# Channel MLP in a fused FAVOR / gated-MLP / mixer kernel: the c additions ahead in VectorE's order, weight sums and last differences on VectorE, the second group's cw loads in pieces, u of the first chunk asked for earlier

## The chip, the cores and the metric

The kernel runs on one core of a Trainium2 chip. The metric is the time of one execution in device microseconds (us). The timed runs of the kernel before gave 1591.82, 1593.74 and 1594.99 us, with the median at 1593.74 us; these come from executions without a profile. One further execution was profiled, and everything said of engines below is from that one.

## The reference

Three stages follow each other, all in float32, over a batch of 8 with 576 tokens and 512 features. The first is a linear attention with exponential features, the second a gated MLP whose gate mixes the tokens, the third a mixer, of which the last part is the channel MLP that this change is about.

```python
def _moe2_ref(x, U, V, w_ch1, w_ch2):
    xt = x.transpose(0, 2, 1)
    h = xt @ U @ V
    u = x + h.transpose(0, 2, 1)
    ch = np.maximum(u @ w_ch1, 0.0) @ w_ch2
    return (u + ch).astype(np.float32)

def reference(**kwargs):
    attn_out = _attn_ref(**attn_kwargs)                # 8 x 8 heads x 576 x 64
    x = np.ascontiguousarray(attn_out.transpose(0, 2, 1, 3)).reshape(B, S, H * D)
    x = _moe_ref(x=x, **moe_kwargs)                    # gated MLP, 512 -> 1024 -> 512
    return _moe2_ref(x=x, **moe2_kwargs)               # low rank token mix, then 512 -> 2048 -> 512
```

## The kernel before

TensorE (PE) works in single-pass float32 (fp32r). Each fp32 operand is split into a rounded part and a rest, and a product of two operands is three matmuls (method `products`, L873). The split (method `split`, L184 to L187) is a cast on ScalarE (ACT) for the rounded part, and a subtraction on VectorE (DVE) for the rest, called the low part below.

**The channel MLP** works through 16 chunks n. A chunk is one batch (576 tokens) with one half of the 2048 hidden features: chunks 0 to 7 take the first group of four weight blocks m (128 x 2 columns each), chunks 8 to 15 the second group. Both matrix products of a chunk are done by a Strassen-like scheme with 7 instead of 8 block products (tables `PRODUCTS` and `OUTER`), so operands need sums and differences of their blocks first. In detail:

- **The right parts** of the first product (method `right_parts`, tiles `t`, `us`): differences of the blocks of the mixer's output u, on GpSimd (POOL, method `less`, L1245), split into `us0` to `us6`. For chunk 0, `first_chunk` (L1241) loads u from the scratch tensor `ud`, and the generator `first_parts` hands out the parts step by step.
- **The first product** (generator `hidden`, tiles `ph_x`, `ph_y`, `ph_z`): 7 products for each weight block, with weights `cw` that `load_left` (L1182) brings in, one load of 1792 KB for each block. DVE adds what PE left in PSUM to copies that ACT made (`c`, L1317). The addition that matters here is the one in `plus(Y, u3, True)`: product 5 of the same block writes into the same bank `ph_z`, so PE must wait until this addition has read it. It is not emitted where it arises, but handed to `inner` as a function (`after`), which `inner` calls one slot later, behind what that slot's caller put on DVE.
- **The second product** (method `channel`, tiles `pc`): operands `hc` (split from the hidden values `h` or their differences `t2`, made by `sums` through `less` on POOL), weights `w` loaded from `w2d` (`outer_weights`, L1449). Its results are added to `r` on DVE (`more`, L1481), stored to `pd` between the groups, and to `outT` at the end.
- **The second group's weights** are prepared while chunks 0 to 6 run (generator `second_group`): 8 blocks, for each four raw 128x256 pieces (tile `ca`), four sums and differences on POOL (`left_sums`, L548, tile `cs`), then splits (tile `cd`, ACT cast and DVE low part) and stores to `w1x` or `w2d` (L1228).

PE runs the two products interleaved, slot by slot: six matmuls of a `ph`, then six of a `pc`, and so on; a chunk has 28 slots of each. Two slots of the table `order` in `inner` are done early: chunk 0's first blocks run in between the last batch's gated output, its low-rank step (`pr`, operands `xh` and `xl`, L1060 and L1062) and its mixing step. The gated MLP and this transition are inside a manual schedule, and the order of instructions on each engine is the order in which the code emits them. DMAs are issued by SyncE (SP) alone, which works in order: a load that waits holds what stands behind it.

`inner` decides by two tables, `begin` (for chunk 1) and `spread` (for the others), at which slots the right parts of the next chunk are made; in the chunk that ends the first group, it calls `load_left` for the four blocks of the second, at slot 6 of each block.

## Time and profile before

| | us |
|---|---|
| timed runs, median (range) | 1593.74 (1591.82 to 1594.99) |
| the profiled execution, own time | 1598.42 |
| the profiled execution, span of the trace | 1596.6 |
| attention (start to about 375) | 375 |
| gated MLP, 8 batches (375 to about 835) | 460 |
| transition and channel MLP (835 to the end) | 762 |

| engine | busy us | share of the span |
|---|---|---|
| PE | 1556.6 | 97% |
| PE weight loads | 1467.3 | 92% |
| DVE | 1133.2 | 71% |
| ACT | 875.8 | 55% |
| POOL | 812.0 | 51% |

PE is the engine that is nearly always busy. In a trace like this, the time that a change can give back is the time that PE does not work or works at the lower of its clock levels, and both are read from PE's rows: each row has its start, its length and in brackets the idle time ahead of it and the instruction that ended it. The granted clock stands in a column of its own in the table of stretches, 1.00 being full speed (2.4 GHz) and 0.5 the lower level (1.2 GHz); a value between says that the stretch had both.

### The profile page before, as it was taken

The page shows a single profiled execution, that of the slowest core. Times are in us where ns is not written, and L with a number is a line of the kernel's source. Part 1 is how long each engine was busy: PE and PEld are TensorE (multiplying, and loading weights), DVE is VectorE, ACT ScalarE, POOL GpSimd, SP SyncE. Part 2 cuts the span into 40 slices and gives each one's busy share as a digit, 9 for nine tenths or more (in the row PEclk, how much of TensorE's full clock was granted, in tenths as well). Part 3 has the DMA queues.
Part 4 walks back from the last instruction along what each step waited for, and adds up shares of the span by engine and source line. Part 5 has one row for each costly group of instructions (what it writes and reads, how often), then busy time and mean ns, then how long its engine had stood idle before and what let it go on. Part 6 is the DMA issues. An engine that isn't in the chain of part 4 may idle for free.

```text
span 1596.6 us, 30554 instructions
## 1 busy us (share of the span) xinstructions
PE 1556.6 (97%) x11592; PEld 1467.3 (92%) x11592; DVE 1133.2 (71%) x1628; ACT 875.8 (55%) x1656; POOL 812.0 (51%) x610
## 2 busy tenths in 40 slices
PE   7999999999999999999999999999999999999998
PEld 7998889988898898898898999999999999999998
DVE  5888767884686787787676767777766666666656
ACT  4878777784444454454445555555544555555542
POOL 2677776766344454453332645455644543434433
PEclk9999999999999999999999999999999999999999
DMA  4677676763243454452328888988989877777786
GB/s 130 172 212 205 195 199 174 205 173 110 83 159 109 129 178 145 139 181 94 110 88 318 258 290 281 317 289 293 311 311 389 259 248 235 237 242 245 248 250 230
DMA packets 172278, 336.87 MB, mean 211 GB/s; under 512 B 25826, under 2 KB 96610, under 8 KB 169060
## 3 DMA queue, kind: packets, MB, share of 16 engines
q1 hardware_dynamic: 171988, 334.86, 65.5%
q8 instruction: 91, 1.49, 0.4%
q14 instruction: 55, 0.45, 0.1%
q10 hardware_dynamic: 144, 0.07, 0.0%
HBM read 251.73 MB, written 73.55 MB: 204 GB/s over the span
## 4 chain that ended last, share of the span: by engine, by line
PE 80%; DMA 8%; DVE 5%; ACT 3%; issue 2%; SPq 1%; POOL 0%; DVEq 0%; ACTq 0%; POOLq 0%
PE pc L873 18%; PE ph_x L873 11%; PE pu L873 6%; PE pz L873 6%; PE pv L873 6%; PE ph_z L873 6%; PE px L873 5%; PE pn L706 4%; PE pkv L678 4%; PE ph_y L873 3%; DMA w<-w2d 2%; PE pk L605 2%; PE pt L637 1%; PE pt L1082 1%; PE pz L1008 1%
## 5 line engine op out<-in xcount | busy, mean ns | idle before, releaser
L873 PE MATMUL pc<-hc,w 128*128 128x288 f32 x2688 | 424.0, 295 | 4.8 <-DMA w<-w2d 2.0
L873 PEld LDWEIGHTS pc<-hc,w 128*128 128x128 f32 x2688 | 379.7, 188 | 6.2 <-ACT us L184 2.0
L659 POOL TENSOR_TENSOR qp<-e,qp 128x576 fp32r<-128x576 f32 x128 | 183.6, 1456 | 119.5 <-ACT e L656 87.3
L873 PE MATMUL ph_x<-us,cw 128*128 128x288 f32 x1536 | 243.0, 296 | 1.1 <-ACT u L1312 0.6
L873 PEld LDWEIGHTS ph_x<-us,cw 128*128 128x128 f32 x1536 | 217.0, 188 | 2.3 <-ACT u L1312 1.4
L706 PE MATMUL pn<-qp,kv 128*65 128x288 f32 x768 | 208.3, 332 | 8.0 <-DVE nd L715 4.4
L187 DVE TENSOR_TENSOR hc<-h,hc 128x576 fp32r<-128x576 f32 x192 | 189.0, 987 | 35.4 <-ACT hc L184 35.3
L1245 POOL TENSOR_TENSOR h<-h,h 128x576 f32<-128x576 f32 x64 | 109.2, 1708 | 132.4 <-DVE r L1481 126.2
L1245 POOL TENSOR_TENSOR t<-u,t 128x576 f32<-128x576 f32 x32 | 56.4, 1762 | 194.9 <-DVE c L1317 179.7
L678 PE MATMUL pkv<-v,kp 128*128 128x65 f32 x1024 | 154.2, 254 | 0.0
L678 PEld LDWEIGHTS pkv<-v,kp 128*128 128x128 f32 x1024 | 152.9, 193 | 0.0
L1312 ACT COPY u<-ph_x 128x288 f32<-128x288 f32 x128 | 51.1, 399 | 184.6 <-PE ph_x L873 184.6
L873 PE MATMUL ph_z<-us,cw 128*128 128x288 f32 x768 | 123.3, 296 | 10.1 <-DVE c L1317 10.1
L184 ACT CAST hc<-h 128x576 fp32r<-128x576 f32 x192 | 128.5, 672 | 6.5 <-PE pc L873 3.6
L1327 ACT ACTIVATE h<-c 128x288 f32<-128x288 f32 x192 | 85.2, 444 | 85.1 <-DVE c L1317 85.0
L873 PEld LDWEIGHTS ph_z<-us,cw 128*128 128x128 f32 x768 | 108.4, 188 | 12.3 <-DVE c L1317 12.2
L706 PEld LDWEIGHTS pn<-qp,kv 128*65 128x65 f32 x768 | 100.1, 141 | 14.1 <-DVE nd L715 6.0
L873 PE MATMUL pz<-wt,vn 128*128 128x288 f32 x768 | 112.0, 295 | 0.0
L873 PEld LDWEIGHTS pz<-wt,vn 128*128 128x128 f32 x768 | 105.3, 188 | 0.0
L1481 DVE TENSOR_TENSOR r<-pc,r 128x576 f32<-128x576 f32 x111 | 83.7, 754 | 30.2 <-PE pc L873 29.6
L873 PEld LDWEIGHTS pu<-xs,wi 128*128 128x128 f32 x768 | 102.7, 188 | 0.7
L873 PE MATMUL pu<-xs,wi 128*128 128x288 f32 x768 | 103.2, 295 | 0.0
(162 smaller groups left out, 3076.2 us busy)
## 6 DMA issues: line engine op xcount, KB each, us to landing
w<-w2d SPq DMA_DIRECT2D x224, 512.0 KB, 4.7
u<-ud SPq DMA_DIRECT2D x16, 1152.0 KB, 8.3
raw_c<-in_w_ch SPq DMA_DIRECT2D x32, 512.0 KB, 3.8
cw<-w1x SPq DMA_DIRECT2D x8, 1792.0 KB, 14.5
v<-in_v SPq DMA_DIRECT2D x32, 325.0 KB, 4.2
k<-in_kT SPq DMA_DIRECT2D x32, 320.0 KB, 3.6
q<-in_qT SPq DMA_DIRECT2D x32, 320.0 KB, 3.9
x<-nd SPq DMA_DIRECT2D x64, 144.0 KB, 3.3
```

Source lines behind the costliest of these rows:

```text
L184: self.put(nc.scalar.copy(hi, src))
L187: return self.put((nc.gpsimd if elo == "pool" else nc.vector).tensor_tensor(out=lo, in0=src, in1=hi, op=ALU.subtract))
L605: self.pin(nc.tensor.matmul(pa[:, j * NF + t, :], x[d, t * P : (t + 1) * P], ws[d, :], start=True, stop=True,))
L637: self.pin(nc.tensor.transpose(pt[:, at, :], s[:, u, :], self.ident))
L659: self.pin(nc.gpsimd.tensor_tensor(out=lo[:, c], in0=e[:, c], in1=hi[:, c], op=ALU.subtract))
L678: self.pin(nc.tensor.matmul(pkv[:, i, j, :], kp[:, j * NF + t, :], vb[:, u * D1 : (u + 1) * D1], start=False, stop=(j == 1 and t == NF - 1),))
L706: self.pin(nc.tensor.matmul(pn, kv[k][:, i, g // 2, :], qp[q][:, i, g * HS : (g + 1) * HS], start=(m == 0), stop=(m == len(terms) - 1),))
L873: self.put(self.nc.tensor.matmul(out, x, y, start=(start and i == 0), stop=(stop and i == len(terms) - 1), skip_group_check=chained,))
L1245: x = self.put(self.nc.gpsimd.tensor_tensor(out=out, in0=p, in1=q, op=ALU.subtract))
L1312: self.put(nc.scalar.copy(out, src))
L1327: self.put(nc.scalar.activation(self.h[n, t // 2, x][:, t % 2], src, AF.Relu))
L1481: self.read = self.put(nc.vector.tensor_tensor(out=r, in0=pc, in1=r, op=ALU.add)).ins
```

## The change

- `first_chunk` is called in the last batch's `gate`, behind the batch's last `pu` products, when its home (tile `xs`) is free; before, it was called when the gate was done.
- `first_parts` hands out the first chunk's right parts in another order and more in each step, so that `us0`, `us4`, `us1` and `us2` stand ahead of the `xh` and `xl` of the low-rank step.
- The addition of `ph_z` and `u3` is marked urgent: `inner` holds it in `self.urgent`, and `hurry` emits it at the head of the next slot or of the next `pc` product, ahead of the `hc` parts, rather than behind them.
- The four sums of each of the 8 blocks are made on DVE instead of POOL. The raw pieces and the sums share one tile `c32`, the splits one tile `cd`, both in the pool `cst`.
- The second group's `cw` come in four pieces for each block (two of 512 KB, two of 384 KB), one asked for at every second slot. Block 4 gets a home of its own, in `c32` and `cd`; block 5 takes the home of block 0, and so on.
- In the last chunk the differences of the hidden values are made on DVE instead of POOL, and the bank pair of the last chunk's first `pc` product is two banks of the tag "a", each added by an instruction of its own.
- The table `begin` makes chunk 1's right parts some slots earlier.

```diff
         )):
-            self.put(self.nc.gpsimd.tensor_tensor(out=z[:, x], in0=p, in1=q, op=op))
+            self.put((engine or self.nc.gpsimd).tensor_tensor(out=z[:, x], in0=p, in1=q, op=op))
...
         loads = [load(kk) for kk in range(2)]
+        if b + 1 == self.B:
+            self.u0 = self.first_chunk()
         gs = self.gs if b == 0 else self.gated(b)
...
                 self.alloc_channel(ctx)
-                u = self.first_chunk()
                 for m in range(GROUP):
                     self.load_left(m)
-                right_parts = self.first_parts(u)
+                right_parts = self.first_parts(self.u0)
                 inner = self.inner()
...
             begun = [self.gated_open(b, t) for t in range(3)]
-            parts(3)
+            parts(4)
             self.work(b, "x")
...
                 ts.append(self.gated_out(b, t, begun[t] if t < 3 else None))
-                parts(1)
+                if t >= 2:
+                    parts(1)
                 if t == 1:
...
-    def load_left(self, m):
+    def load_left(self, m, whole=True):
         g, t = divmod(m, GROUP)
-        w = self.cw.tile([P, 2, 7, 2, P], F32R, tag=f"w{t}", name=f"cw{m}", bufs=1)
-        self.nc.sync.dma_start(
-            w.bitcast(F32).rearrange("p i x k c -> p i x (k c)"), self.w1x[g][:, t]
-        )
-        self.w1[m] = w
+        dma = self.nc.sync.dma_start
+        if whole:
+            w = self.cw.tile([P, 2, 7, 2, P], F32R, tag=f"w{t}", name=f"cw{m}", bufs=1)
+            dma(w.bitcast(F32).rearrange("p i x k c -> p i x (k c)"), self.w1x[g][:, t])
+            self.w1[m] = [w[:, i] for i in range(2)]
+            return
+        if t == 0:
+            self.w1[m] = [
+                self.cst.tile([P, 16 * P], F32R, tag=tag, name=f"cw{m}_{tag}", bufs=1)[:, : 14 * P]
+                .rearrange("p (x k c) -> p x k c", x=7, k=2) for tag in ("c32", "cd")
+            ]
+        else:
+            w = self.cw.tile([P, 2, 7, 2, P], F32R, tag=f"w{t - 1}", name=f"cw{m}", bufs=1)
+            self.w1[m] = [w[:, i] for i in range(2)]
+        def load(i, x):
+            dma(
+                self.w1[m][i].bitcast(F32)[:, x].rearrange("p x k c -> p x (k c)"),
+                self.w1x[g][:, t][:, i, x],
+            )
+        self.pieces += [
+            lambda i=i, x=x: load(i, x) for x in (slice(0, 4), slice(4, 7)) for i in range(2)
+        ]
...
     def fetch_raw(self, kind, m):
-        a = self.cst.tile([P, 4, 2 * P], F32, tag="c32a", name=f"ca{kind}_{m}", bufs=1)
+        a = self.c32[:, 0].rearrange("p (x c) -> p x c", x=4)
         return self.raw_blocks(a, kind, m)
-    def sums_of(self, a, name):
-        z = self.cst.tile([P, 4, 2 * P], F32, tag="c32s", name=f"cs{name}", bufs=1)
-        self.left_sums([a[:, x] for x in range(4)], z)
+    def sums_of(self, a):
+        z = self.c32[:, 1].rearrange("p (x c) -> p x c", x=4)
+        self.left_sums([a[:, x] for x in range(4)], z, self.nc.vector)
         return z
...
         blocks = [(kind, m) for kind in (1, 2) for m in range(GROUP, self.NM)]
+        self.c32 = self.cst.tile([P, 2, 8 * P], F32, tag="c32", name="c32", bufs=1)
+        self.cd, made = self.cst.tile([P, 2, 8 * P], F32R, tag="cd", name="cd", bufs=1), 0
         raw = self.fetch_raw(*blocks[0])
...
             t, a = m - GROUP, raw
-            z = self.sums_of(a, f"{kind}_{m}")
+            z = self.sums_of(a)
             yield
             for x, k, src in ((0, 2, a[:, :2]), (2, 1, a[:, 2:3]), (3, 2, z[:, :2]), (5, 2, z[:, 2:])):
-                d = self.w2p.tile([P, 2, 2, 2 * P], F32R, tag="cd", name=f"cd{kind}_{m}_{x}", bufs=2)
+                d = self.cd[:, made % 2].rearrange("p (i k c) -> p i k c", i=2, k=2)
+                made += 1
                 self.split(d[:, 0, :k], d[:, 1, :k], src, elo="dve")
...
-    def less(self, out, p, q, after=None):
-        x = self.put(self.nc.gpsimd.tensor_tensor(out=out, in0=p, in1=q, op=ALU.subtract))
+    def less(self, out, p, q, after=None, engine=None):
+        engine = engine or self.nc.gpsimd
+        x = self.put(engine.tensor_tensor(out=out, in0=p, in1=q, op=ALU.subtract))
         if after is not None:
...
         parts = self.right_parts(0, u)
-        for names in (("t1", "t2"), (0,), (4,), (2,), ("t3",), (1,), ("t6",), (3,), (6,), (5,)):
+        for names in (("t1", "t2", 0), ("t3", 4), (1,), ("t6", 2), (3,), (6,), (5,)):
             for x in names:
...
         c22 = []
-        yield lambda: c22.append(plus(Y, u3, True))
+        def add():
+            c22.append(plus(Y, u3, True))
+        add.urgent = True
+        yield add
         product(X, 6, False, True)
...
         begin = {
-            (1, 4): ("t1", "t2"), (2, 2): ("t3",), (2, 3): (0,), (2, 6): (4,), (3, 2): (1, "t6"),
-            (3, 3): (2,), (3, 4): (3,), (4, 0): (6,), (3, 6): (5,),
+            (1, 4): ("t1", "t2"), (2, 0): ("t3",), (2, 1): (0,), (2, 2): (4,), (2, 3): (1, "t6"),
+            (2, 4): (2,), (2, 5): (3,), (2, 6): (6,), (3, 6): (5,),
         }
...
                 late = None
+            self.hurry()
             after = next(pairs[k])
...
             late = after
+            if getattr(after, "urgent", False):
+                self.urgent, late = after, None
             if (t, i) == (1, 0) and n + 1 < groups * B:
...
                 right.pop(x)()
-            if i == 6 and (n + 1) % B == 0 and g + 1 < groups:
-                self.load_left((g + 1) * GROUP + t)
+            if (n + 1) % B == 0 and g + 1 < groups and (i == 6 and t < GROUP - 1 or (t, i) == (0, 0)):
+                self.load_left((g + 1) * GROUP + (t + 1 if i else 0), False)
+            if self.pieces and i % 2 == 0:
+                self.pieces.pop(0)()
             yield
+        self.hurry()
         if late:
             late()
+    def hurry(self):
+        f, self.urgent = self.urgent, None
+        if f:
+            f()
...
         b11, b12, b21, b22 = (self.h[n, q, i] for i in range(4))
+        last = n + 1 == self.NM // GROUP * self.B
+        engine = self.nc.vector if last else None
         if x == 1:
-            self.less(b11, b12, b11, after)
+            self.less(b11, b12, b11, None if last else after, engine)
         elif x == 2:
             self.t2[n, q] = self.hc.tile([P, 2, self.HS], F32, tag="t2", name=f"t2{n}_{q}", bufs=2)
-            self.less(self.t2[n, q], b22, b11)
+            self.less(self.t2[n, q], b22, b11, engine=engine)
         elif x == 3:
-            self.less(b12, b22, b12)
+            self.less(b12, b22, b12, engine=engine)
         else:
-            self.less(b21, b21, self.t2[n, q])
+            self.less(b21, b21, self.t2[n, q], engine=engine)
...
             r = rs[n, i, j]
+            if isinstance(pc, list):
+                for f in range(2):
+                    self.put(nc.vector.tensor_tensor(out=r[:, f], in0=pc[f], in1=r[:, f], op=ALU.add))
+                return
             self.read = self.put(nc.vector.tensor_tensor(out=r, in0=pc, in1=r, op=ALU.add)).ins
...
                 if x in (0, 4, 2):
-                    pc = banks(f"pc{n}_{x}", "x" if x == 0 else "y")
+                    if x == 0 and n + 1 == total:
+                        pc = [self.psum(f"pc{n}_{x}_{f}")[:, :HS] for f in range(2)]
+                    else:
+                        pc = banks(f"pc{n}_{x}", "x" if x == 0 else "y")
                     if x == 0:
...
                             r = rs[n, 1, 0][:, f]
-                            self.put(nc.vector.tensor_tensor(out=r, in0=X[:, f], in1=r, op=ALU.add))
+                            self.put(nc.vector.tensor_tensor(out=r, in0=X[f], in1=r, op=ALU.add))
                             store(n, 1, 0, (f,))
...
                 for t in range(GROUP):
+                    self.hurry()
                     if t % 2 == 0:
...
                         self.products(
-                            pc[:, f],
+                            pc[f] if isinstance(pc, list) else pc[:, f],
                             [([w[:, t % 2, i, f * P : (f + 1) * P] for i in range(2)],
```

On DVE, at the start of the channel MLP, the order before was this (`us` are right parts, `xh` and `xl` the operands of the low-rank step):

```order
L187 TENSOR_TENSOR us0_0_9742<-u32_0_9698,us0_0_9742 128x576
L187 TENSOR_TENSOR us4_0_9745<-u32_0_9698,us4_0_9745 128x576
L186 CAST xh7_0_9749<-x_7_0_9748 128x512
L187 TENSOR_TENSOR xl7_0_9750<-x_7_0_9748,xh7_0_9749 128x512
L187 TENSOR_TENSOR us2_0_9757<-t1_0_9738,us2_0_9757 128x576
L186 CAST xh7_1_9761<-x_7_1_9760 128x512
L187 TENSOR_TENSOR xl7_1_9762<-x_7_1_9760,xh7_1_9761 128x512
L186 CAST xh7_2_9771<-x_7_2_9770 128x512
L187 TENSOR_TENSOR xl7_2_9772<-x_7_2_9770,xh7_2_9771 128x512
L187 TENSOR_TENSOR us1_0_9779<-t2_0_9740,us1_0_9779 128x576
L186 CAST xh7_3_9783<-x_7_3_9782 128x512
L187 TENSOR_TENSOR xl7_3_9794<-x_7_3_9782,xh7_3_9783 128x512
```

The order after the change:

```order
L187 TENSOR_TENSOR us0_0_9742<-u32_0_9512,us0_0_9742 128x576
L187 TENSOR_TENSOR us4_0_9746<-u32_0_9512,us4_0_9746 128x576
L187 TENSOR_TENSOR us1_0_9749<-t2_0_9740,us1_0_9749 128x576
L187 TENSOR_TENSOR us2_0_9753<-t1_0_9738,us2_0_9753 128x576
L186 CAST xh7_0_9757<-x_7_0_9756 128x512
L187 TENSOR_TENSOR xl7_0_9758<-x_7_0_9756,xh7_0_9757 128x512
L186 CAST xh7_1_9766<-x_7_1_9765 128x512
L187 TENSOR_TENSOR xl7_1_9767<-x_7_1_9765,xh7_1_9766 128x512
L186 CAST xh7_2_9775<-x_7_2_9774 128x512
L187 TENSOR_TENSOR xl7_2_9776<-x_7_2_9774,xh7_2_9775 128x512
L187 TENSOR_TENSOR us3_0_9783<-u32_0_9512,us3_0_9783 128x576
L186 CAST xh7_3_9787<-x_7_3_9786 128x512
```

The right parts `us1` and `us2` moved ahead of all `xh` and `xl`, and `us3` from behind them to ahead of the last two.

On DVE, in chunk 1 (products `pc1` beside `ph2`), around the addition of block 1, which is the row `c2_1` with `u32_1`, before:

```order
L187 TENSOR_TENSOR hc1_1_0_10970<-t21_0_10888,hc1_1_0_10970 128x576
L187 TENSOR_TENSOR cd1_5_0_11002<-ca1_5_10427,cd1_5_0_11002 128x512
L187 TENSOR_TENSOR cd1_5_2_11007<-ca1_5_10427,cd1_5_2_11007 128x256
L187 TENSOR_TENSOR hc1_1_1_11017<-t21_1_10967,hc1_1_1_11017 128x576
L1317 TENSOR_TENSOR c2_1_11037<-ph2_1_z_10981,u32_1_11000 128x288
```

After the change:

```order
L187 TENSOR_TENSOR hc1_1_0_10964<-t21_0_10882,hc1_1_0_10964 128x576
L187 TENSOR_TENSOR cd_10254<-c32_10253,cd_10254 128x512
L187 TENSOR_TENSOR cd_10254<-c32_10253,cd_10254 128x256
L1341 TENSOR_TENSOR c2_1_11008<-ph2_1_z_10975,u32_1_10994 128x288
L187 TENSOR_TENSOR hc1_1_1_11010<-t21_1_10961,hc1_1_1_11010 128x576
```

The addition moved from behind `hc1_1_1` to ahead of it; the two `cd` rows still stand ahead.

On DVE, in chunk 0 (products `pc0` beside `ph1`), around the addition of block 3, `c1_3` with `u31_3`, before:

```order
L1317 TENSOR_TENSOR c1_3_10659<-ph1_3_y_10652,s11_3_10604 128x288
L187 TENSOR_TENSOR us1_2_10680<-t2_2_10543,us1_2_10680 128x576
L187 TENSOR_TENSOR hc0_5_1_10689<-h3_0_2_10182,hc0_5_1_10689 128x576
L187 TENSOR_TENSOR us2_2_10707<-t1_2_10531,us2_2_10707 128x576
L1481 TENSOR_TENSOR r0_11_10328<-pc0_0_10262,r0_11_10328 128x576
L187 TENSOR_TENSOR us3_2_10726<-u32_2_10341,us3_2_10726 128x576
L187 TENSOR_TENSOR hc0_6_0_10729<-h2_0_0_9910,hc0_6_0_10729 128x576
L1317 TENSOR_TENSOR c1_3_10749<-ph1_3_z_10700,u31_3_10724 128x288
```

After the change:

```order
L1341 TENSOR_TENSOR c1_3_10654<-ph1_3_y_10647,s11_3_10602 128x288
L187 TENSOR_TENSOR us1_2_10675<-t2_2_10540,us1_2_10675 128x576
L548 TENSOR_TENSOR c32_10253<-c32_10253 128x256 x4
L187 TENSOR_TENSOR hc0_5_1_10683<-h3_0_2_10188,hc0_5_1_10683 128x576
L187 TENSOR_TENSOR us2_2_10701<-t1_2_10528,us2_2_10701 128x576
L1527 TENSOR_TENSOR r0_11_10331<-pc0_0_10263,r0_11_10331 128x576
L187 TENSOR_TENSOR us3_2_10720<-u32_2_10342,us3_2_10720 128x576
L1341 TENSOR_TENSOR c1_3_10723<-ph1_3_z_10694,u31_3_10718 128x288
L187 TENSOR_TENSOR hc0_6_0_10725<-h2_0_0_9910,hc0_6_0_10725 128x576
```

Four sums (`c32<-c32`, one row, x4) came in ahead of the addition, and `hc0_6_0` went behind it. Chunk 5 has its second block of sums at the same place.

On SP, in chunk 6's second product, around the last store of a split (`w2d1<-cd`), before:

```order
L1449 DMA w2_6_3_1_14037<-w2d0_87 128x1024
L1449 DMA w2_6_5_0_14079<-w2d0_87 128x1024
L1228 DMA w2d1_88<-cd2_7_5_14112 128x2x256 x2
L1449 DMA w2_6_5_1_14120<-w2d0_87 128x1024
L1182 DMA cw6_14156<-w1x1_90 128x3584
L1449 DMA w2_6_6_0_14161<-w2d0_87 128x1024
L1449 DMA w2_6_6_1_14204<-w2d0_87 128x1024
L1494 DMA pd6_84<-r6_11_13893 128x2x288
L1449 DMA w2_7_0_0_14244<-w2d0_87 128x1024
```

After the change:

```order
L1199 DMA cw6_13977<-w1x1_90 128x1024
L1491 DMA w2_6_5_0_14044<-w2d0_87 128x1024
L1199 DMA cw6_13977<-w1x1_90 128x768 x2
L1251 DMA w2d1_88<-cd_10254 128x2x256 x2
L1491 DMA w2_6_5_1_14086<-w2d0_87 128x1024
L1199 DMA cw7_14122<-w1x1_90 128x1024
L1199 DMA cw4_cd_13645<-w1x1_90 128x1024
L1199 DMA cw4_cd_13645<-w1x1_90 128x768
L1491 DMA w2_6_6_0_14127<-w2d0_87 128x1024
L1199 DMA cw7_14122<-w1x1_90 128x1024
L1491 DMA w2_6_6_1_14171<-w2d0_87 128x1024
```

Of block 4, the half that lies in `cd` is asked for right behind the last store out of `cd`; the pieces of blocks 6 and 7 stand between the `w2` loads one at a time.

## Rows read from the trace of the kernel before

**Rows 1.** Waits of PE from 835 us on: us in total, times, longest.

```profile
PE ph_z L873 <- DVE c L1317: 10.1, 9, 2.6
PE pc L873 <- DMA w<-w2d: 2.0, 2, 1.8
PE pc L873 <- DVE r L1481: 1.3, 2, 0.9
```

**Rows 2.** Stretches: span, busy us of PE, PEld, DVE, ACT, POOL, clock, DMA.

```profile
851.00:855.50 4.50, 4.32 (x20) 3.92 (x20) 4.26 (x7) 1.55 (x3) 1.54 (x1) 0.62 0.99 421
884.00:888.50 4.50, 4.50 (x25) 4.50 (x24) 3.34 (x6) 3.35 (x8) 0.13 (x1) 0.63 0.66 215
1164.00:1259.00 95.00, 90.63 (x680) 89.77 (x679) 61.84 (x85) 47.23 (x102) 40.01 (x24) 1.00 0.92 330
1259.00:1526.00 267.00, 267.00 (x2021) 267.00 (x2020) 169.13 (x241) 137.31 (x294) 119.48 (x72) 1.00 0.79 246
```

**Rows 3.** Timeline, transition: start, length, engine, line, operation, count, idle before.

```profile
835.91 0.32 SPq L529 DMA_DIRECT2D w2r<-w_c  x1
...
836.33 0.37 SPq L1241 DMA_DIRECT2D u<-ud  x1
...
842.11 1.25 ACT L184 CAST us<-u 128x576 fp32r<-128x576 f32 x2 [4.41 <-DMA u<-ud]
...
847.95 0.50 PE L1060 MATMUL pr<-xh,ua 128*128 128x512 f32 x1 [0.24 <-DVE xh L186]
...
852.06 1.64 PE L873 MATMUL ph_x<-us,cw 128*128 128x288 f32 x6
```

**Rows 4.** Timeline, chunk 0, the longest wait of PE.

```profile
883.65 1.07 PE L873 MATMUL ph_z<-us,cw 128*128 128x288 f32 x6 [2.65 <-DVE c L1317]
```

**Rows 5.** Timeline, chunk 6, block 1: the low part of hc, c, PE.

```profile
1178.72 1.96 DVE L187 TENSOR_TENSOR hc<-t,hc 128x576 fp32r<-128x576 f32 x1
...
1181.10 1.06 PE L873 MATMUL ph_z<-us,cw 128*128 128x288 f32 x6 [1.73 <-DVE c L1317]
```

**Rows 6.** Timeline, chunk 3, block 3: the same place, other wait.

```profile
1064.59 0.75 DVE L187 TENSOR_TENSOR hc<-h,hc 128x576 fp32r<-128x576 f32 x1
...
1065.76 1.06 PE L873 MATMUL ph_z<-us,cw 128*128 128x288 f32 x6 [1.28 <-DVE c L1317]
```

**Rows 7.** Timeline, chunk 0, block 3: c, and PE that takes it.

```profile
925.25 0.45 DVE L1317 TENSOR_TENSOR c<-ph_z,u 128x288 f32<-128x288 f32 x1
...
926.61 0.96 PE L873 MATMUL ph_z<-us,cw 128*128 128x288 f32 x6
```

**Rows 8.** Durations by line, 880 to 1200 us: ns least, median, most.

```profile
L187 DVE TENSOR_TENSOR cd<-ca,cd x16: 412/904/1921, 898.7 to 1177.1; 128x512 fp32r<-128x512 f32 x8, 128x256 fp32r<-128x256 f32 x8
...
L548 POOL TENSOR_TENSOR cs<-ca x16: 722/747/1317, 892.8 to 1148.9; 128x256 f32<-128x256 f32 x16
```

**Rows 9.** Timeline, chunk 6: loads on SP, and the wait for w.

```profile
1192.06 1.10 SPq L1228 DMA_DIRECT2D w2d<-cd  x2
...
1194.61 2.63 SPq L1449 DMA_DIRECT2D w<-w2d  x2
...
1199.13 1.03 PE L873 MATMUL pc<-hc,w 128*128 128x288 f32 x6 [1.76 <-DMA w<-w2d]
```

**Rows 10.** DMA issues, 1160 to 1235 us: KB each, median us to landing.

```profile
w<-w2d SPq DMA_DIRECT2D x22, 512.0 KB, 10.0
cw<-w1x SPq DMA_DIRECT2D x4, 1792.0 KB, 11.2
...
w2d<-cd SPq DMA_DIRECT2D x6, 256.0 KB, 6.0
```

**Rows 11.** Timeline, the last product of the kernel.

```profile
1567.68 8.51 PE L873 MATMUL pc<-hc,w 128*128 128x288 f32 x61 [0.90 <-issue]
1567.72 1.82 POOL L1245 TENSOR_TENSOR h<-h,h 128x576 f32<-128x576 f32 x1 [28.12 <-DVE r L1481]
...
1576.80 1.73 PE L873 MATMUL pc<-hc,w 128*128 128x288 f32 x11 [0.61 <-DVE hc L187]
...
1579.46 3.43 PE L873 MATMUL pc<-hc,w 128*128 128x288 f32 x24 [0.93 <-DVE r L1481]
```

More of the change, by code (lines that the diff above doesn't have):

```diff
@@ L175, in __init__ @@
         self.w1x = [dp.tile([P, GROUP, 2, 7, 2 * P], F32, name=f"w1x{g}") for g in range(2)]
-        self.pinning = False
+        self.pinning, self.urgent, self.pieces = False, None, []
     def psum(self, name, tag="a"):
@@ L538, in work, with left_sums @@
             f()
-    def left_sums(self, blocks, z):
+    def left_sums(self, blocks, z, engine=None):
         a11, a12, a22, a21 = blocks
@@ L1303, in product @@
                 [
-                    ([w[:, i, l, k, :] for i in range(2)], [u[:, i, k, :] for i in range(2)])
+                    ([w[i][:, l, k, :] for i in range(2)], [u[:, i, k, :] for i in range(2)])
                     for k in range(2)
```

## The prediction

> **What bounds the kernel now.** I read the page first: PE is busy for 97% of the span, so a gain can only come from places where PE waits or runs at the lower clock. Second, the stretches: from 1259 to 1526 us PE is busy for 267.00 of 267.00 us [rows 2], so the second half of the channel MLP has nothing to give, and faster work elsewhere on DVE or POOL is worth nothing there. Third, the waits of PE behind 835 us [rows 1]: 10.1 us in nine waits for DVE's `c` and 2.0 us for `w`. Fourth, the timeline at each. Everything that the change can reach lies in the transition, in chunks 0 to 8 and in the last product.
>
> **The change part by part.** Terms are gains in us, from the profiled execution.
>
> (a) *The start of the channel MLP.* Chunk 0's u is asked for at 836.33, behind the `w2r` store, and ACT begins the right parts at 842.11 after 4.41 us of idling for that load [rows 3]. Asked for behind the last `pu`, u is there well before; the parts can then start at about 838 (behind the store, whose tile the new pool may reuse), some 4 us sooner, and the order on DVE puts them ahead of `xh` and `xl`. What this is worth is read from PE: the six `pr` matmuls from 847.95 to the first `ph_x` at 852.06 take 4.11 us [rows 3]. In the steady part 2021 matmuls of 288 columns take 267 us [rows 2], 0.132 each; six of 512 columns would take 6 x 0.132 x 512/288 = 1.41. So 2.7 us are lost to `xh` and `xl` coming late. Behind this, from 851 to 855.5, the clock is 0.62, that is, part of the stretch at 1.2 GHz [rows 2]: 4.32 busy us x 0.38 = 1.6 more. Together 4.3 at most. The least is what remains if `xh` and `xl` stay late behind the parts and only the clock holds better: 1.2, an estimate from half of the 2.7 being lost anew. I take 3.5, nearer the upper end, since DVE idles there until the load comes.
>
> (b) *The longest wait, chunk 0.* At 883.65 PE has waited 2.65 us for `c` [rows 4], and the stretch 884 to 888.5 has a clock of 0.63 [rows 2]: 4.5 x 0.37 = 1.7. The addition is now emitted ahead, and the right parts that delay it come earlier. Between 0 (the parts are just as dense) and 4.3; I take 2.5.
>
> (c) *c ahead.* Eight waits remain, 10.1 - 2.65 = 7.45 us. They are of two kinds. Four, 2.98 together, have the low part of `hc` directly ahead of `c` on DVE; the longest is 1.73, with an `hc` of 1.96 [rows 5]. The addition now goes ahead of that `hc`, which is longer than each of these waits or about as long: gain 2.98. Three more, 4.23 together (1.28 in [rows 6]), stand behind a row of split parts and additions, of which only the last, an `hc` of 0.75 [rows 6], goes behind: 3 x 0.75 = 2.2. One of 0.25 keeps its order. So 5.2. What goes behind `c` is later by 0.45, the length of `c` [rows 7], and nothing shows that PE would notice: outside the last product no wait for `hc` is among the waits of PE.
>
> Against this stand the sums, 8 x 4 instructions of 128x256. On POOL one takes 747 ns in the median; on DVE the nearest row, a subtraction of two SBUF operands at widths of 256 and 512, runs from 412 to 1921 ns [rows 8]. I take 0.55, near the lower end, because the short form is half of the width of the long one and POOL has less to do: 2.2 for a block. In chunk 0, block 3 (and likewise chunk 5) the four stand ahead of `c`, while an `hc` of 0.75 leaves. Before, `c` ends at 925.70 and PE takes it at 926.61, 0.91 of slack [rows 7]. So 2.2 - 0.75 - 0.91 = 0.54 late, twice: 1.1. In chunk 0, block 1 I allow 0.3. The other blocks of sums stand behind `c` or where DVE idles ahead of it. Net: 5.2 - 1.4 = 3.8. The bounds: 7 with sums at 412 ns and POOL out of the way; 0 with sums at 1 us, 5 x 1.0 late.
>
> A page of the Trainium skill bears on this: GPSIMD Engine Reference, section Performance versus the Vector engine, has an add on GpSimd at 1.96 times the time on VectorE. By it a sum would take 0.38, below the least row of 412 ns, and the term (c) would be 1.3 more. No run shows a sum on DVE yet.
>
> (d) *cw in pieces.* The two waits for `w` are 2.0 us [rows 1], the long one 1.76 at 1199.13 [rows 9], while loads of 512 KB land after 10.0 us beside `cw` loads of 1792 KB [rows 10]. With pieces at most 512 KB stand ahead of a `w` where it was 1792. But the order on SP has a new wait: the half of block 4 that lies in `cd` waits until the last store out of `cd` has landed, and `w` loads stand behind it. That store is issued at 1192.06 to 1193.16 and such stores take 6.0 to land [rows 9, 10], so the next `w`, at 1194.61 before, would go out at about 1199, up to 4.2 later. Less is queued ahead of it then, so I take half of the range: old waits 2.0 gone, 1.0 new. Gain 1.0, between -3 and 2.0.
>
> Here too a page speaks, and against the change: the Trainium skill, DMA: Bandwidth & Descriptors, section Rules for kernel authors, says that splitting a transfer or spreading it brings no bandwidth, as all run on the same 16 engines. The share of the DMA engines is 0.92 from 1164 to 1259 [rows 2]. If `w` is late for bytes and not for its place in the queue, (d) is 0 and the time 1.0 more.
>
> (e) *The last product.* PE stands 0.90 at 1567.68 (it resumes as the bank of `pc` comes free of the last addition), 0.61 for an `hc` at 1576.80 that waits for POOL's differences of 1.82, and 0.93 for `r` at 1579.46 [rows 11], 2.4 together. Separate banks take the first away; differences on DVE, at the 0.75 of an `hc` of the same width [rows 6] in place of 1.82 and with POOL quiet, most of the others. DVE gets eight more instructions, some 6 us, which take the place of its idling for POOL. Between 0 and 2.4; I take 2.0.
>
> Costed at nothing: the new tables' instructions (the same number on PE), and the chunk 1 parts moved earlier, whose DVE time is the same.
>
> Sum: 3.5 + 2.5 + 3.8 + 1.0 + 2.0 = 12.8. The profiled execution, 1598.42, would be 1585.6. It is 0.3% above the median of the timed runs, 1593.74; the waits should be the same there, so the forecast is 1593.74 - 12.8 = 1580.9, say 1581.
>
> **The rivals.**
>
> *The sums come dear (slower).* DVE shares its work with POOL, and rows of the same form reach 1921 ns [rows 8]. At 1.2 us a sum, four take 4.8 in place of the 0.91 + 0.75 that there is room for: 3.1 late at each of five blocks that have their sums ahead of `c`, 15.7; each such wait is longer than the 2.65 that brought the lower clock and 1.7 more [rows 2, 4], so 8.4. With 14.2 of gains without the sums: 1593.74 - 14.2 + 24.1 = 1603.6. It decides from about 1.0 us for one sum; 3.0 must then be lost at five places. For it: an `hc` of 1.96 [rows 5], against 0.75 [rows 6], shows that such instructions can double in length. Against: `hc` in one of the worst places has its short length, 0.75 [rows 6], and POOL loses 32 instructions. 5 in 100. The Trainium skill, GPSIMD Engine Reference, section Key points, names the mechanism: the SBUF interface is shared and instructions with two SBUF inputs contend. The row of 412 to 1921 ns agrees that it exists, not that it lasts.
>
> *The start stays where it is.* u is early, but the parts still begin late, as their tiles wait for what the closed pool last did, or PE meets `cw`, which lands late with it. Then (a) and (b) are 0: 1593.74 - 6.8 = 1587. For it: the DMA engines are full from 851 on, at 0.99 [rows 2]. Against: 4.41 us of idling for this one load. 17 in 100.
>
> *SP stands still.* The wait for `cd` costs PE the whole 4.2 and 1.7 of clock: (d) is 2.0 - 5.9 = -3.9, the time 1593.74 - 7.9 = 1586. 18 in 100.
>
> **How the numbers follow.** The forecast, 1581, has 60 in 100. If all upper ends held, 4.3 + 4.3 + 7 + 2.0 + 2.4 = 20, the time would be 1574; the rivals of a partial gain end at 1587, both together at 1592. Eight in ten lie between 1574, which all terms at their best would give, and 1590. A measurement of this kernel tells some 0.2%, 3.2 us, from no change, so faster means below 1590.5. The forecast and most of the two partial rivals lie there: 0.86; within 0.2%: 0.08, both partial rivals together or a smaller loss to the sums; slower 0.06.
>
> **What would show it.** (a): `ph_x` follows six `pr` without idling, at clock 1.00 by 851 on the trace's time. (b), (c): waits of PE for `c` fall from 10.1 to about 4, sums on DVE near 0.55. (d): waits for `w` below 1.5 in chunk 6, SP idling ahead of the `cw` piece for `cd`. (e): PE idles under 1 us behind 1562. Wrong would be: sums at 1 us or above; a new wait of PE for `hc` or `w` of more than 4 us; the parts of chunk 0 starting at 842 as before.

## The result and the profile after

The changed kernel is slower. Timed beside each other, six runs each: 1602.17 us after (1600.29 to 1608.19) and 1595.36 us before, ratio 1.0056 with a 95% interval of 1.0041 to 1.007. Forecast were 1581 us and a gain of 12.8. The profiled execution of after took 1603.02 us, with a span of 1601.2; that of before took 1598.42.

The waits of PE from 835 us on, after the change (us in total, times, longest), answer to [rows 1]:

```profile
PE ph_z L873 <- DVE c L1341: 9.4, 3, 4.5
PE ph_x L873 <- DMA cw_cd<-w1x: 6.3, 1, 6.3
PE ph_x L873 <- ACT u L1336: 1.9, 4, 0.8
PE pc L873 <- DMA w<-w2d: 1.2, 1, 1.2
PE pc L873 <- DVE hc L187: 0.8, 2, 0.5
PE pc L873 <- DVE us L187: 0.4, 1, 0.4
```

Nine waits for `c` became three, with nearly the same total: two of them last 4.46 us. And a wait stands there that before had no counterpart, 6.3 us for the half of `cw` that lies in `cd`. The name in the last row is a coincidence: a `pc` product reads no `us`, and the load of `w` that this one reads landed at the same moment, 1200.31, so it is a wait for `w`.

PE issues 11592 matmuls in both kernels. The table takes places in the trace of before, and gives by how much the matmul with the same number starts later in the trace of after, and what the stretch ahead of it added. The first stretch, up to 835 us, is the part of the program that the change doesn't touch; executions differ there by some us.

| place in before, us | after against before, us | added in the stretch | what lies in it |
|---|---|---|---|
| 835 | -2.2 | -2.2 | attention, gated MLP |
| 860 | -5.9 | -3.7 | the start, term (a) |
| 890 | -10.2 | -4.3 | chunk 0, its long wait, term (b) |
| 935 | -8.7 | +1.5 | chunk 0, first block of sums |
| 1040 | -11.2 | -2.5 | chunks 1 to 3, c ahead |
| 1060 | -7.5 | +3.7 | chunk 3, sums |
| 1114 | -4.5 | +3.0 | chunk 4, sums |
| 1140 | +1.7 | +6.2 | chunk 5, sums |
| 1185 | -0.3 | -1.9 | chunk 6, c ahead |
| 1215 | +7.3 | +7.6 | chunk 7 into 8, `cw` |
| 1562 | +7.0 | -0.3 | second half |
| 1590 | +4.7 | -2.3 | last product, term (e) |

From 835 us on, the negative stretches add up to 15.0 us; the prediction had 14.2 of gains without the sums. The positive ones add up to 22.0: 14.4 where the sums stand, 7.6 at `cw`. The difference, 6.9, is that of the medians, 6.8.

**The sums.** The timeline of after, in chunk 4 (start, length, engine and line, operation, count, idle before):

```profile
1076.34 1.89 POOL L1269 TENSOR_TENSOR h<-h,h 128x576 f32<-128x576 f32 x1
...
1076.86 6.28 DVE L548 TENSOR_TENSOR c<-c 128x256 f32<-128x256 f32 x4
...
1078.19 1.59 POOL L1269 TENSOR_TENSOR u<-u 128x576 f32<-128x576 f32 x1
...
1079.74 3.12 POOL L1269 TENSOR_TENSOR h<-h,t 128x576 f32<-128x576 f32 x2
1083.06 0.45 DVE L1341 TENSOR_TENSOR c<-ph_z,u 128x288 f32<-128x288 f32 x1
...
1083.56 1.30 PE L873 MATMUL ph_z<-us,cw 128*128 128x288 f32 x6 [4.46 <-DVE c L1341]
```

Four sums last 6.28 us, 1.57 each, and four GpSimd instructions lie beside them, the last ending at 1082.86. Then the addition runs in 0.45, and PE has stood 4.46 us. The view of one line over all 32 sums (ns least, median, most) and two stretches (span, busy us with counts of PE, PEld, DVE, ACT, POOL, clock, DMA share and GB/s) show that this hangs on GpSimd:

```profile
L548 DVE TENSOR_TENSOR c<-c x32: 410/426/1655, 888.5 to 1154.8; 128x256 f32<-128x256 f32 x32
```

```profile
1076.86:1083.06 6.20, 2.24 (x17) 2.01 (x16) 6.17 (x6) 1.86 (x4) 6.00 (x4) 1.00 0.86 265
912.98:914.53 1.55, 1.55 (x14) 1.55 (x13) 1.52 (x6) 0.77 (x3) 0.00 (x0) 1.00 0.83 271
```

At 913, where GpSimd did nothing (0.00), four sums took 1.55 us in total, 0.42 each. At 1077 GpSimd was busy for 6.00 of 6.20 us. A sum is either 0.42 or about 1.6. Over all 32 in the trace of after, the 18 that have no GpSimd instruction beside them last 0.41 to 0.43, and the 14 that have one last 1.30 to 1.66; none lies between. Chunks 0 (first block), 4 and 5 (first block) have all four of the long kind, chunk 3 two. In chunk 3 PE waits for no more than 0.17, 0.27 and 0.77 us, but the clock falls behind these waits too, where before it was 1.00:

```profile
1040.50:1045.00 4.50, 4.50 (x26) 4.50 (x26) 2.09 (x4) 2.02 (x6) 0.00 (x0) 0.70 0.98 340
```

**The half of cw in cd.** The timeline of after from 1195 us:

```profile
1195.18 0.96 SPq L1251 DMA_DIRECT2D w2d<-cd  x2
...
1197.52 0.33 SPq L1199 DMA_DIRECT2D cw<-w1x  x1
...
1204.06 0.80 SPq L1199 DMA_DIRECT2D cw_cd<-w1x  x2
1204.91 0.42 SPq L1491 DMA_DIRECT2D w<-w2d  x1
...
1208.02 0.61 PE L873 MATMUL ph_x<-us,cw_cd 128*128 128x288 f32 x1 [6.28 <-DMA cw_cd<-w1x]
```

The last store out of `cd` went out at 1195.18 to 1196.14. SP then stood from 1197.85 to 1204.06 until it had landed, and only then could issue the load into `cd`, which landed at 1207.98. PE wanted it at about 1201.7. The waits of SP from 1190 to 1210 us name the store:

```profile
SPq L1199 <- DMA w2d<-cd: 6.2, 1, 6.2
```

The lower clock added to each. The stretches of after behind the wait in chunk 4 and behind the wait for `cw`, and the one that answers to the second of [rows 2]:

```profile
884.00:888.50 4.50, 4.50 (x36) 4.50 (x36) 2.38 (x4) 3.05 (x7) 4.42 (x4) 1.00 0.95 284
...
1083.00:1087.50 4.50, 3.94 (x18) 3.94 (x19) 3.47 (x7) 1.44 (x3) 0.00 (x0) 0.63 0.46 133
1208.00:1214.00 6.00, 5.98 (x25) 5.98 (x26) 0.76 (x1) 1.72 (x4) 0.00 (x0) 0.51 1.01 352
```

At 884 the clock is back at 1.00, where before it was 0.63 [rows 2]; at 1083 and 1208 it is now 0.63 and 0.51, that is, mostly 1.2 GHz.

### The profile page after: what moved, and what is told of

Read it like the earlier page. It is cut to its first block, busy times and chain, and to the rows that moved or that the text cites. A ratio compares the mean times of both kernels' runs of the same rounds, so it can differ in the third digit from the quotient of the medians.

```text
span 1601.2 us, 30521 instructions
## 1 busy us (share of the span) xinstructions
PE 1557.6 (97%) x11592; PEld 1470.2 (92%) x11592; DVE 1161.3 (73%) x1671; ACT 876.4 (55%) x1656; POOL 767.2 (48%) x570
## 4 chain that ended last, share of the span: by engine, by line
PE 83%; DMA 6%; DVE 4%; ACT 3%; issue 2%; POOL 1%; SPq 1%; ACTq 0%; DVEq 0%; POOLq 0%
PE pc L873 20%; PE ph_x L873 11%; PE pu L873 6%; PE pz L873 6%; PE ph_z L873 6%; PE pv L873 6%; PE px L873 5%; PE pn L706 5%; PE pkv L678 4%; PE ph_y L873 3%; PE pk L605 2%; PE pt L637 1%; PE pt L1084 1%; PE pq L605 1%; PE pz L1010 1%
## 5 line engine op out<-in xcount | busy, mean ns | idle before, releaser
L873 PE MATMUL ph_x<-us,cw 128*128 128x288 f32 x1344 | 214.2, 296 | 2.0 <-ACT u L1336 1.9
L873 PEld LDWEIGHTS ph_x<-us,cw 128*128 128x128 f32 x1344 | 190.8, 189 | 3.5 <-ACT u L1336 3.3
L1269 POOL TENSOR_TENSOR t<-u,t 128x576 f32<-128x576 f32 x32 | 59.7, 1866 | 267.1 <-DVE c L1341 216.6
L1269 POOL TENSOR_TENSOR h<-h,h 128x576 f32<-128x576 f32 x60 | 99.8, 1665 | 118.7 <-DVE r L1527 115.2
L873 PE MATMUL ph_z<-us,cw 128*128 128x288 f32 x672 | 109.0, 298 | 9.6 <-DVE c L1341 9.4
L873 PEld LDWEIGHTS ph_z<-us,cw 128*128 128x128 f32 x672 | 95.9, 190 | 11.0 <-DVE c L1341 10.7
```

The source lines that it names most:

```text
L873: self.put(self.nc.tensor.matmul(out, x, y, start=(start and i == 0), stop=(stop and i == len(terms) - 1), skip_group_check=chained,))
L1269: x = self.put(engine.tensor_tensor(out=out, in0=p, in1=q, op=ALU.subtract))
```

## The experiments

Theory A says: beside a busy GpSimd, one VectorE instruction with two SBUF operands passes for each GpSimd instruction, and the second loss is the store that the load into `cd` waits for. Its rivals stand in each expectation.

**e1: the sums back on GpSimd.**

```diff
-        self.left_sums([a[:, x] for x in range(4)], z, self.nc.vector)
+        self.left_sums([a[:, x] for x in range(4)], z)
```

> The changed kernel with the weight sums back on GpSimd, nothing else changed. Theory A (a sum on VectorE beside a busy GpSimd lasts about 1.6 us whatever its width; in chunks 0, 3, 4 and 5 four of them stand ahead of the addition that PE waits for): the two waits of 4.46 us and the lower clock behind them go, time 1602.2 - (1.5 + 3.7 + 6.1 + 6.2) = about 1585; some is given back where GpSimd's sums are late. Rival B (the two long waits come from the new order of c and hc, or from VectorE's load in general): with the sums gone VectorE has 10 to 20 us less to do but the waits stay above 2 us each, time above 1595. The wait of 6.28 us for the half of cw in cd stays in both.

Measured: 1585.23 us (1582.46 to 1590.93) against 1594.58 before, ratio 0.9942 (0.9919 to 0.9965). Its waits of PE from 835 us on:

```profile
PE ph_x L873 <- DMA cw_cd<-w1x: 6.2, 1, 6.2
PE pc L873 <- DMA w<-w2d: 3.0, 2, 1.7
PE ph_z L873 <- DVE c L1341: 0.6, 1, 0.6
PE ph_x L873 <- ACT u L1336: 0.4, 1, 0.4
```

The waits for `c` fall from 9.4 to 0.6, with `c` and `hc` in the changed order; the time is that of theory A. So the half of rival B that blames the new order falls. The other half, VectorE's load in general, is not told apart here, as that load is less too; e5 does it.

**e2: own homes for the second group's cw.**

```diff
-            w = self.cw.tile([P, 2, 7, 2, P], F32R, tag=f"w{t - 1}", name=f"cw{m}", bufs=1)
+        w = self.cw.tile([P, 2, 7, 2, P], F32R, tag=f"w{t}", name=f"cw{m}", bufs=1)
...
-                self.load_left((g + 1) * GROUP + (t + 1 if i else 0), False)
+                self.load_left((g + 1) * GROUP + t, False)
```

> The changed kernel, but each block of the second group's cw goes into the home of the block with the same number of the first group, still in four pieces; no home in c32 and cd. Theory A (the load into cd waits on SP for the landing of the last store out of cd, and PE for that load): the wait of 6.28 us at 1201 and the lower clock behind it go, time 1602.2 - 7.6 = about 1594.6, and the longest wait for w stays under 2 us. Rival B (the DMA engines are full there and bytes decide): a wait of similar size for w or cw shows up within 20 us of that place, time above 1599.

Measured: 1596.17 us (1592.49 to 1601.41), ratio to before 0.9998 (0.9978 to 1.0018), so 6.0 below the changed kernel, of 7.6 expected. The wait for `cw_cd` is gone, the long waits for `c` stay, and of the waits for `w` one is longer than theory A had it:

```profile
PE ph_z L873 <- DVE c L1335: 9.3, 3, 4.5
PE pc L873 <- DMA w<-w2d: 4.5, 2, 2.7
```

Rival B falls: its wait within 20 us is not there, and the time is below 1599. The longer one, 2.73, is in the last product. The other (1.75 us, from 1229) stands behind the pieces, so part of what the home cost comes back as a wait for `w`.

**e3: both.** The two diffs together.

> Both at once: sums on GpSimd and own homes. If the two losses are separate and are all that went wrong, 1602.2 - 17.5 - 7.6 = about 1577, the forecast of the prediction or better. If the gains at the start and of c ahead were not real, 1590 or above.

Measured: 1577.38 us (1574.97 to 1578.43) against 1594.58, ratio 0.9879 (0.9841 to 0.9916). This is 3.6 below the forecast of the prediction. Its waits of PE from 835 us on that are above 0.5 us:

```profile
PE pc L873 <- DMA w<-w2d: 3.3, 2, 1.7
PE ph_z L873 <- DVE c L1335: 0.6, 1, 0.6
```

Without both parts the time is 24.8 below the changed kernel, where e1 and e2 alone have 16.9 and 6.0, 22.9 together. So the two losses are separate within what these runs tell, and they are all that made the change slower.

**e4: each sum in two halves.**

```diff
-            self.put((engine or self.nc.gpsimd).tensor_tensor(out=z[:, x], in0=p, in1=q, op=op))
+            for c in ((slice(0, P), slice(P, 2 * P)) if engine else (slice(None),)):
+                self.put((engine or self.nc.gpsimd).tensor_tensor(out=z[:, x, c], in0=p[:, c], in1=q[:, c], op=op))
```

> The changed kernel with each weight sum as two instructions of half the width (128 columns), 64 in place of 32, the same elements. Theory A (beside a busy GpSimd one VectorE instruction passes for each GpSimd instruction): in the crowded blocks of chunks 4 and 5 an instruction still lasts 1.4 to 1.7 us, as long as GpSimd is busy, so PE waits longer there, the waits going from 4.46 towards 6 to 10 us each; time 1605 to 1615. Rival B (contention stretches each element): an instruction lasts about 0.8 us, a block's sums stay at 6.3 us, time 1602 to 1604. In the quiet blocks an instruction goes from 0.42 to about 0.28 in both.

One run, 1607.61 us. The sums' line, then the timeline of e4 in chunk 4 with two stretches of it:

```profile
L549 DVE TENSOR_TENSOR c<-c x64: 276/281/1520, 892.3 to 1158.4; 128x128 f32<-128x128 f32 x64
```

```profile
1080.09 6.55 DVE L549 TENSOR_TENSOR c<-c 128x128 f32<-128x128 f32 x8
1081.42 1.47 POOL L1270 TENSOR_TENSOR u<-u 128x576 f32<-128x576 f32 x1
1082.85 2.84 POOL L1270 TENSOR_TENSOR h<-h,t 128x576 f32<-128x576 f32 x2
...
1087.07 1.32 PE L874 MATMUL ph_z<-us,cw 128*128 128x288 f32 x5 [4.71 <-DVE c L1342]
```

```profile
1080.09:1085.76 5.67, 2.27 (x18) 2.04 (x16) 5.67 (x5) 1.89 (x4) 5.60 (x4) 1.00 0.91 270
1085.76:1086.57 0.81, 0.00 (x0) 0.00 (x0) 0.81 (x6) 0.00 (x0) 0.00 (x0) 1.00 0.03 9
```

An instruction of half the width still lasts up to 1520 ns beside GpSimd; theory A's mechanism holds, and rival B's stretching of each element falls. Within the first stretch four halves pass beside four GpSimd instructions; GpSimd then has nothing more to do, and the other four take 0.81 together. For this reason PE's wait grows only from 4.46 to 4.71: the consequence that I drew from theory A, 6 to 10 us, was wrong. Here the wait ends with GpSimd's work, not with the number of VectorE instructions. The time, inside the range of theory A, is no evidence for it: by PE's matmuls e4 is 3.8 us later at 835 already, ahead of any change, and 4.6 at the end, so it costs under 1 us against the changed kernel.

**e5: the sums on VectorE, but where GpSimd is idle** (own homes as in e2).

```diff
-                        for _ in range({5: 2, 6: 1, 13: 1, 14: 1, 17: 1}.get(at, 0)):
+                        for _ in range(PULLS[n].get(at, 0)):
+PULLS = (
+    {5: 2, 6: 1, 13: 1, 14: 1, 17: 1}, {5: 2, 6: 1, 13: 1, 14: 1, 17: 1}, {5: 2, 6: 1, 13: 1, 14: 1, 17: 1},
+    {5: 2, 13: 1, 14: 1, 15: 1, 17: 1}, {5: 1, 13: 1, 14: 1, 15: 1, 17: 1},
+    {5: 1, 13: 1, 14: 1, 15: 1, 17: 1}, {5: 1, 13: 1, 14: 1, 15: 1, 17: 1, 18: 1},
+)
```

> The changed kernel with own homes for the second group's cw (as in e2) and the sums on VectorE, but from the fifth block on the sums stand at slot 13 of a chunk, behind the addition for the third block, where GpSimd is idle in the trace. Theory A (what costs is one VectorE instruction waiting for each GpSimd instruction): all sums but the first block's last 0.42 us, the waits of 4.46 go, time that of e3 plus 1.5 to 2 for the first block in chunk 0: 1577.4 + 2 = about 1579. Rival B (a sum on VectorE costs its place in the queue wherever it stands): a wait for c of 1 us or more in most of chunks 3 to 6, time 1585 or above.

Measured: 1583.02 us (1579.58 to 1588.14), ratio 0.9932 (0.9909 to 0.9956). Its sums and its waits of PE:

```profile
L553 DVE TENSOR_TENSOR c<-c x32: 412/418/1659, 891.4 to 1176.6; 128x256 f32<-128x256 f32 x32
```

```profile
PE pc L878 <- DMA w<-w2d: 3.7, 2, 2.5
PE ph_x L878 <- ACT u L1335: 1.3, 3, 0.6
PE ph_z L878 <- DVE c L1340: 0.7, 2, 0.4
PE pc L878 <- DVE hc L192: 0.6, 1, 0.6
```

All sums but those of the first block are short, and the waits for `c` are 0.7: same engine, same instructions, other place. So theory A holds for the length of a sum and for the waits, and B falls. The time is 4 us above the expectation, outside it, and below B's 1585. By PE's matmuls the profiled execution of e5 is 1.6 us later than e3's at 845, ahead of any sum, and 5.3 at 1590. Of the 3.7 between, 1.6 are at the first block, as expected. Another 1.4 come between 935 and 1040, half of them two waits for `u` that e3 doesn't have. From there to 1200 e5 gets 1.3 back, and it loses 2.3 again up to 1230, where it waits longer for `w` (2.55 us, e3 1.70). Why, no run tells.

**e6, e7, e8: one part alone, on the kernel before.** e6 has the urgent addition (`add.urgent`, `hurry`), e7 `first_chunk` in `gate` with the new `first_parts` and `begin`, e8 the last chunk's differences on VectorE with its two banks; the diffs are the lines of the change.

> The kernel before with the addition of ph_z and u3 alone moved ahead of the hc parts. Term (c) of the prediction without the sums is 5.2: 1594.6 - 5.2 = about 1589. If the wait for c only turns into a wait for hc or for the next part, 1593 or above.

> The kernel before with the start alone changed: u asked for in the last batch's gate, the new order of the first parts and the new table begin. The trace of the changed kernel shows 3.6 and 4.3 us gained between 845 and 890: 1594.6 - 8 = about 1586.5. The rival, that the gain needs the addition ahead as well (in chunk 0): 3.6 alone, about 1591.

> The kernel before with the last chunk alone changed: differences on VectorE and two separate banks for the first pc. Term (e) of the prediction: 1594.6 - 2.0 = about 1592.6; the trace of the changed kernel shows 2.3 gained behind 1562, with a wait of 1.2 for w in it. If the loads of w take the place of the old waits, 1594.

| | us | ratio to before, interval | by PE's matmuls |
|---|---|---|---|
| e6, c ahead | 1589.99 | 0.998 (0.996 to 1.0001) | 1.9 between 860 and 890, 4.7 from there to 1185 |
| e7, start | 1588.91 | 0.996 (0.9944 to 0.9976) | 3.6 up to 860, 4.0 to 890 |
| e8, last chunk | 1592.92 | 0.9989 (0.9973 to 1.0004) | 2.5 behind 1562 |

e7 is a gain by its interval, 5.7 us in the medians where 8 were expected; the start gains without the addition ahead, against the rival. For e6 and e8 the intervals reach 1, so that the time alone doesn't tell them from no change; their traces have PE earlier at the places named and nowhere later by as much. In e6 the four waits with an `hc` ahead of `c` are gone, and no wait for `hc` takes their place; the three behind a row of split parts are 0.7 shorter each (0.98, 0.61 and 0.61 left). The waits for `u` grow from 0.6 to 1.5.

**e9, e10: are the pieces worth anything?** e9 is e3 with whole loads, e10 is e3 once more beside it.

```diff
-                self.load_left((g + 1) * GROUP + t, False)
+                self.load_left((g + 1) * GROUP + t)
```

> e3 (sums on GpSimd, own homes) with the second group's cw in whole loads of 1792 KB at the places of the kernel before, to see what the pieces are worth. If a w waits for the bytes queued ahead of it: a wait for w of 1.7 us or more near 1200, as in the kernel before, time 0 to 3 us above e3, 1577 to 1581. If the number of loads counts and not their size (SP waits for an earlier landing before it issues again): as in e3 or better, 1575 to 1577.

> The kernel of e3 again, on the same chip as e9, for the comparison: 1577 within 0.2%.

Measured: 1578.18 us whole (1575.03 to 1578.92) and 1578.85 in pieces (1573.53 to 1589.57); ratios to before 0.9903 (0.9886 to 0.9919) and 0.9908 (0.9875 to 0.9941). In time, no difference that these runs tell. In the profiled executions PE waits at other places. The two longest kinds of e9, the second of them in the timeline, and the load of `w` issued at 1168.41:

```profile
PE pc L873 <- DMA w<-w2d: 2.2, 1, 2.2
PE pc L873 <- ACT us L184: 1.4, 1, 1.4
```

```profile
1178.19 1.03 PE L873 MATMUL pc<-hc,w 128*128 128x288 f32 x6 [1.43 <-ACT us L184]
```

```profile
DMA to landing us min/median/max: 9.6/9.6/9.6
```

The first wait is in the last product. The second has the wrong name again: a `pc` product reads no `us`. The load of `w` landed at 1178.06, 0.13 ahead of the product. By count this is the matmul that waited 1.76 for `w` at 1199.13 in before [rows 9], 0.14 behind the landing of its load. So the wait of before is back with the whole loads, 1.43 long, though the first expectation said 1.7 or more; e6, e7 and e8, whole as well, have 1.2 to 1.3 there. In e9 the `w` was issued behind a `cw` of 1792 KB and landed 2.2 behind it.

With pieces this product does not wait in any run. There a later one waits for `w`: 1.70 in e3, 1.75 in e2, 2.55 in e5, 3.48 in e10, where whole loads have at most 0.45. In e3 that `w` went out at 1199.49, and SP had stood for an earlier load of `w` that landed at 1199.43; for an earlier landing it stood before each issue from 1191 to 1203 us. One line of SP's waits in e3 from 1185 to 1215 us:

```profile
SPq L1485 <- DMA w<-w2d: 1.9, 2, 0.9
```

So both expectations are seen in these traces, each in its place: with whole loads `w` is late behind the bytes ahead of it, with pieces behind the number of loads. The pieces moved the wait and did not make the kernel faster.

## Why the prediction was wrong

- **What bounds the kernel**: right. Everything happened in the stretches named, and the second half changed by 0.3 us.
- **(a) and (b)**, 3.5 and 2.5 forecast: 3.7 and 4.3 in the trace. The parts start at 835.75, as soon as the `w2r` store has landed; after is 2.2 us ahead of before there, so this is the 838 that was said. PE runs into `ph_x` at 847.43: the six `pr` matmuls take 2.1 us in place of 4.1, and the clock from 851 to 855.5 is 1.00 in place of 0.62. The clock at 884 stays up, so (b) came to its upper end. The rival that the start stays where it is fell. By e7 chunk 1's earlier parts and the new order alone give 4.0 of (b), by e6 the addition ahead alone 1.9; together they give 4.3.
- **(c), the addition ahead**, 5.2 forecast: 4.7 in e6, and 8.9 between 890 and 1185 in e3. The mechanism was right. Part of why it is more in e3 than in e6 is seen in the traces: at two of the waits that e6 keeps (0.98 and 0.61), a low part on DVE ahead of `c` lasts 1.92 and 1.99 us beside GpSimd in e6, and 0.68 and 0.74 with GpSimd idle in e3, where both waits are gone. Why GpSimd's instructions lie elsewhere in e3, no run tells.
- **(c), the sums**, 1.4 us of loss forecast: some 17 in e1's median. Here the prediction failed. The step was the price of one sum: 0.55 us, chosen "near the lower end" of one row that ran from 412 to 1921 ns [rows 8]. That row was not a range about a middle, it was two kinds at each of its widths, short with GpSimd idle and long with GpSimd busy; the choice had to be made for each place, by what GpSimd does there. Its sentence "the other blocks of sums stand behind `c` or where DVE idles ahead of it" was wrong with it: the first blocks of chunks 4 and 5 stand ahead of `c` and beside four GpSimd instructions, and lasted 6.3 us each. Of the places that the prediction did price, block 3 of chunks 0 and 5 cost nothing, as GpSimd is idle there and the sums took 0.42; chunk 0's first block, allowed 0.3, cost 1.5. The halving of width by which 0.55 was reached has no meaning in the crowded places, as e4 shows.
- **The rival of the dear sums** named the mechanism and the sign, at 1.2 us and five blocks; it was 1.6 at three blocks and a half. It was given 5 in 100. That its 1603.6 lies so near the 1602.17 measured is luck: it had 24.1 lost to the sums, where they cost some 17, and the rest is the loss at `cw`, which it doesn't contain. The row for it (an `hc` of 1.96 beside GpSimd) was in hand, and the argument against it (an `hc` of 0.75 elsewhere) was no argument about the places that count.
- **The Trainium skill**, GPSIMD Engine Reference, section Key points, on the shared interface: the trace agrees, with 0.42 against 1.6. Its factor of 1.96 between the engines (section Performance versus the Vector engine) is 1.8 in the quiet places here, 747 ns on GpSimd [rows 8] against 418 in e5's median on VectorE, so that here the measured 1.8 counts. In the crowded ones VectorE took twice GpSimd's time.
- **(d)**, a gain of 1.0 forecast: a loss of 7.6. This is the second step that failed. The new wait of SP was seen, but too short: up to 4.2 (its own rows give 4.5, as 1193.16 + 6.0 - 1194.61), where SP stood 6.2, as the store took 8.4 from issue to landing. What was missed is who waits: I charged it to the `w` loads behind it, and not to PE, which needs the load itself. The prediction didn't ask when the first product of chunk 8 starts; it runs ahead of `pc` and wanted its weights at 1201.7. The rival that SP stands still had a cost to PE and the clock, 5.9, through the `w` loads; it was given 18 in 100. No gain from the pieces is seen either, by e9 and e10.
- **(e)**, 2.0 forecast: 2.3 in the trace, 2.5 in e8. The old waits are gone; a wait of 1.24 for `w` stands in the last product instead.

## What to carry to other kernels

An instruction's price on an engine that slows down beside another one is read at the place where it will stand, from what the other engine does at that time; a mean over the kernel hides two prices. When a buffer gets a new tenant, follow the chain of both: the store that must land, the queue that stands meanwhile, and the consumer's first use of the new tenant. Moving the sums off GpSimd, which PE did not wait for, gained nothing here, while the change without it and with own homes for `cw` was 1.2% faster than before (e3; 0.9% in e10). And where the name of a wait is not something that the instruction reads, look for a load that landed at the same moment.

## What the runs showed of the hardware

Beside a busy GpSimd a VectorE instruction with two SBUF operands lasts about as long as one GpSimd instruction, whatever its own width: 128 columns 0.28 us alone and up to 1.52 beside it, 256 columns 0.42 and up to 1.66, 576 columns 0.75 and up to 2.0 (1.96 in [rows 5]). They pass in turn, four beside four. GpSimd pays as well: its 128x576 instructions last 1.43 us in before where no such VectorE instruction lies beside them, and 1.8 to 1.9 in the median where one does. Additions with an operand in PSUM keep their length, 0.44 to 0.46 in before with a GpSimd instruction over all of it (54 of them) or none (35). The timeline of before, chunk 6, has one wholly within a GpSimd instruction:

```profile
1180.02 1.93 POOL L1245 TENSOR_TENSOR u<-u 128x576 f32<-128x576 f32 x1
1180.60 0.45 DVE L1317 TENSOR_TENSOR c<-ph_z,u 128x288 f32<-128x288 f32 x1
```
